# Second MoE's gate and value products by Strassen's block sums: 7 products for 8

## Chip, cores and metric

The kernel runs on one core of one Trainium2 chip. The metric is device time in microseconds (us), from launch to end; lower is better. The median of three runs stands for a kernel, and beside it there is one profiled execution, whose records are what the prediction reads.

## What is computed

Three parts follow each other: an attention with a bias made by a small network, a first mixture of experts (MoE) that takes the maximum of three products, and a second MoE that multiplies a value by a sigmoid gate.

```python
scores = scale * q @ k.T + bias           # batch 4, heads 8, sequence 576, head dim 64
x = softmax(scores) @ v                   # x: 2304 x 512
h = max(x @ w1, x @ w2, x @ w3)           # first MoE, 512 -> 768
x = h @ w_out                             # 768 -> 512
gate = 1 / (1 + exp(-(x @ w_gate)))       # second MoE, 512 -> 1536
val = x @ w_val                           # 512 -> 1536
out = (gate * val) @ w_out                # 1536 -> 512
```

The MoE weights come as 64-bit floats. The kernel decodes them to 32 bits and keeps each as two 16-bit halves, high and low.

## The kernel before

Every large product is done as three 16-bit products (high by high, high by low, low by high) that add up in one PSUM bank. The helper `mm3` (line 929, its matmuls are line 933) issues such three. The sequence of 576 tokens of a batch is worked in two halves of 288 columns, each a bank's worth.

The work is written down by a recorder (class `Recorder`): each call to an engine becomes an item with its dependences, a class of urgency (`BIAS` 0, `ATT` 1, `MOE` 2, `PREP` 3) and a cost estimate (`cost`). `emit` then sets the order on each engine by picking, among the next items of each class, the one that could start first by these estimates. Items recorded under `nc.join()` with two engines may go to either. So the order on each engine is fixed when the program is built, and an engine that comes to an item whose inputs are late waits there, with all that stands behind it.

The stages, in order of time:

- Attention, pairs of heads P = 0 to 15, four pairs per batch. `pair` loads the bias from DRAM on the SP or ACT queue (`am<-bias_d`, line 830), forms scores on TensorE, takes the maximum on VectorE (line 835) and the exponential on ScalarE (line 836). `by_pe` or `by_dma` transposes the probabilities; the DMA transposes run on the SP queue (lines 775 and 862). `value_out` makes the value product (line 878).
- First MoE, `moe1(b)`, of batch b, recorded in class MOE: it fills TensorE in the gaps of the attention of the next batch. Per batch it has 576 matmuls. Its end scales its output x and writes it as two 16-bit halves to the arena tiles `x2[b]` (lines 1008 and 1009), where all four batches stay.
- Weights of the second MoE, `split` (line 1107), after the attention has left the arena `Am`: per matrix and block of 128 columns one DMA, `decode64` (lines 543 to 545, three VectorE instructions of 512 elements), a sum of squares on ScalarE, a power-of-two scale, then the high half on ScalarE (line 1122) and the low half on VectorE (line 1123). There are 12 blocks each of gate and value weights, and 12 pieces of output weights, which need `vrel`, a scale taken from all value weights.
- Second MoE: `gate(b, m)` for 4 batches and 12 blocks m. `prod` makes the gate product and the value product, each 4 x 2 x 3 = 24 matmuls into a pair of banks. ScalarE takes the sigmoid from PSUM (line 1171), VectorE multiplies it by the value product from PSUM (line 1174), ScalarE and VectorE write the two halves (lines 1175 and 1176). `outs` makes the output product of 128 tokens, 36 matmuls of 512 columns (line 1200), put between gates by the table `between`; VectorE scales it out of PSUM (line 1205).

Of the kernel before, what the change touches and what calls it, by code (L numbers as in the profile page):

```python
# [37 lines left out]
class Mem:  # L38
# [7 lines left out]
    def region(self, ap):  # L46
# [75 lines left out]
class Recorder:  # L122
# [5 lines left out]
    DEAR = {"PE": 0.0, "DVE": 0.8, "ACT": 0.0, "POOL": 0.0, "SP": 0.0}  # L128
    NCLS = 4
# [69 lines left out]
    def cost(eng, method, out, reads, kwargs):  # L199

        n = 1
# [4 lines left out]
        if method.startswith("dma"):  # L206
# [8 lines left out]
            return (0.55 if eng == "SP" else 0.1), size / (285e3 if dram else 400e3 if size > 6e5 else 300e3) * (1.6 if parts == 64 and n > 500 else 1.0) + 0.03, 1.85  # L215
# [32 lines left out]
    def start(self, it, e):  # L248

        t = self.t_eng[e]  # L250
        for d in it.deps:
            e2, lat, own = self.ends[d]
            x = own if e2 == e == "PE" else lat
            if x > t:
                t = x
        for i in it.banks:
            for o, x in self.bank[i].items():
                if o != e and x > t:
                    t = x
# [4 lines left out]
    def choose(self, e, lists, force=False):  # L264
# [3 lines left out]
        for c in range(self.NCLS):  # L268
            ks = lists[e][c]
            seen, w = None, 0  # L270
            for it in ks:
# [7 lines left out]
                s = self.start(it, e)  # L279
# [16 lines left out]
    def emit(self):  # L296
# [15 lines left out]
        while left:  # L312
# [8 lines left out]
            calls, (busy, work, lat) = it.alts[e]  # L321
            self.t_eng[e] = s + busy
# [88 lines left out]
SIDE_CLS = ATT  # L411
PE_ALL, PE_SQ = 6, 8
# [30 lines left out]
def tile_kernel(ctx, tc, q, k, v, w1, b1, w2, mw1, mw2, mw3, mwo, gw, vw, ow, xtab, masks, out):  # L443
# [17 lines left out]
    bias_d = dram.tile([S, H, SB], F32, tag="bias_d", name="bias_d")  # L461
    PS = psum.tile([128, 4096], F32, tag="ps", name="ps")
# [29 lines left out]
    x2 = [X2[:, 2304 * b:2304 * (b + 1)].bitcast(F16).rearrange("p (e k s) -> p e k s", e=2, k=KC) for b in range(B - 1)]  # L492
# [74 lines left out]
    def up_down(src, s=None, u=None):  # L567

        g = total(src)
        e = tiny_ap().bitcast(I32)  # L570
# [44 lines left out]
    nc.sync.dma_start(wb[:, 0:1], w1.rearrange("o c -> c o").unsqueeze(0).to_broadcast([4, 32, 1]))  # L615
    nc.sync.dma_start(ytab[:, 3 * NY:], xtab[:, 3 * NY:ny])
    nc.scalar.dma_start(wb[:, 1:2], b1.rearrange("(o c z) -> o c z", o=1, z=1).to_broadcast([4, 32, 1]))
    nc.sync.dma_start(psib, xtab[:, ny + nz:ny + nz + 8 * NTAB])
    nc.sync.dma_start(msk, masks[:, 0:40])
    nc.scalar.dma_start(w2raw, w2.unsqueeze(0).to_broadcast([4, 32, H]))  # L620
# [327 lines left out]
    def moe1(b, xd, mm):  # L948
# [115 lines left out]
    common_scales()  # L1064
    mm_b = Ring([bank(6), bank(7)])
    side = first_weights((3,), Ring([X2[:, 3072 + 1536 * i:4608 + 1536 * i] for i in range(2)]), {3: X2[:, 0:3072]}, square_sum)
    for b in range(1, B):
        for P in range(PPB * b, PPB * b + PPB):
            for it in range(NIT):
# [7 lines left out]
                for _ in range(2):  # L1077
                    prep(u)
                    u += 1
                    if u >= SIDE3:  # L1080
                        next(side, None)
                if it == 1:
                    value_out(P, 0, 256, vb, pt0, True)
            value_out(P, 256, 320, vb, pt1_f if P < PE_ALL else pt1, P < PE_ALL)
            if P == PPB * b:
                with nc.at(MOE):
                    moe1(b - 1, x2[b - 1], mm_b)


    attic = Am[:, 0:3072], Am[:, 3072:7680], Am[:, 7680:13824], Am[:, 13824:19968], Am[:, 19968:22272], Am[:, 22272:23296]  # L1090
    w64_r = Ring([attic[0][:, 1024 * i:1024 * (i + 1)].bitcast(I32).rearrange("p (f t) -> p f t", t=2) for i in range(3)])
    wf_r = Ring([attic[1][:, 512 * i:512 * (i + 1)] for i in range(9)])
    GW, VW = (t.bitcast(F16).rearrange("p (e k f) -> p e k f", e=2, k=KC) for t in attic[2:4])
    x2.append(attic[4].bitcast(F16).rearrange("p (e k s) -> p e k s", e=2, k=KC))
    ob_r = Ring([attic[5][:, 512 * i:512 * (i + 1)] for i in range(2)])
    sg_r = Ring([Wm[:, S * i:S * (i + 1)] for i in range(2)])
    gT = Wm[:, 1152:14976].bitcast(F16).rearrange("p (e k s) -> p e k s", e=2, k=K2)
    OW = Wm[:, 14976:21120].bitcast(F16).rearrange("p (e k f) -> p e k f", e=2, k=K2)

    with nc.at(MOE):  # L1100
        moe1(B - 1, x2[B - 1], Ring([bank(i) for i in (0, 1, 2, 3, 5, 6, 7)]))

    scl = {nm: f32_tile([128, 2, n], nm + "_su") for nm, n in (("gw", K2), ("vw", K2), ("ow", KC))}
    vrel = f32_tile([128, K2], "vrel")
    vmn, vmx = tiny_ap(), tiny_ap()

    def split(nm, m, pieces, rel=False):

        ss = tiny_ap(len(pieces))
        fs = []  # L1110
        for i, (src, hi, lo) in enumerate(pieces):
            t, f = w64_r(), wf_r()
            nc.sync.dma_start(t.rearrange("p (k f) t -> p k f t", k=src.shape[1]), src)
            decode64(f, t)
            fv = f.rearrange("p (k f) -> p k f", k=src.shape[1])
            if rel:
                nc.vector.tensor_tensor(fv, fv, vrel[:, 4 * i:4 * i + 4].unsqueeze(2).to_broadcast([128, 4, 128]), op=ALU.mult)
            square_sum(f, ss[:, i:i + 1])
            fs.append((fv, hi, lo))
        s, _ = up_down(ss, scl[nm][:, 0, m:m + 1], scl[nm][:, 1, m:m + 1])  # L1120
        for fv, hi, lo in fs:
            nc.scalar.activation(hi, fv, AF.Copy, scale=s)
# [140 lines left out]
```

## Time and profile before

| | us |
|---|---|
| median of three runs | 1045.07 |
| lowest, highest | 1040.01, 1052.55 |
| the profiled execution | 1053.29 |
| span of its records | 1051.5 |
| TensorE busy in the span | 1014.2 |
| VectorE busy | 636.0 |
| ScalarE busy | 543.2 |
| GpSimd busy | 114.5 |

The span runs from the first to the last instruction; 1.8 us of the profiled execution lie outside it. PE is TensorE's matmuls, PEld its weight loads, DVE is VectorE, ACT ScalarE, POOL GpSimd, SP the engine that issues most DMAs. A matmul's record covers its way through the array, so matmuls overlap and 48 matmuls of 286 ns may take 6 us. L933 is line 933 of the kernel before. The changed kernel's lines lie 11 further down from line 620 to 950 or so (L830 becomes L841), and L933 becomes L944.

### The profile page before, as it was taken

Reading aid. Unit: us, or ns where it says so; the run is one execution under the profiler, and the core shown is the slowest. Engines: PE = TensorE matmul, PEld = TensorE weight load, DVE = VectorE, ACT = ScalarE, POOL = GpSimd, SP = SyncE. Lnnn points to the kernel's source line nnn. Section 1 sums busy time; section 2 is a strip of 40 time slices with the busy share of each in tenths; the row PEclk is TensorE's granted clock in tenths of the full one; section 3 lists DMA queues with packets and bytes.
Section 4 is the critical chain, followed back from the end, with each engine's and each line's share of the span. In section 5 each row is a group of like instructions: output and inputs, shape, how many; then the busy total and the mean of one; then the engine's idle time right before and its main releaser. Section 6 shows DMA issues by size and latency. Waiting matters only on the chain.

```text
span 1051.5 us, 21090 instructions
## 1 busy us (share of the span) xinstructions
PE 1014.2 (96%) x8326; PEld 687.3 (65%) x8326; DVE 636.0 (60%) x1613; ACT 543.2 (52%) x1142; POOL 114.5 (11%) x141
## 2 busy tenths in 40 slices
PE   5798998999999899999999999999999999999998
PEld 2354576665676666677778777777665666766643
DVE  5799997987888788788999929632211211221110
ACT  5899985786797777877675346422111111211100
POOL 1011132431132123121000100000000000000000
PEclk9999998999999999999999999999999999999999
DMA  7897768576999999979763401000000000000001
GB/s 197 258 306 262 258 185 187 149 190 166 206 240 171 236 223 212 224 141 237 159 190 117 158 19 61 1 1 1 11 21 21 11 11 21 1 11 11 11 21 41
DMA packets 160014, 130.02 MB, mean 124 GB/s; under 512 B 111404, under 2 KB 140332, under 8 KB 159916
## 3 DMA queue, kind: packets, MB, share of 16 engines
q1 hardware_dynamic: 157892, 121.61, 46.3%
q10 hardware_dynamic: 2024, 7.08, 2.7%
q8 instruction: 65, 1.06, 0.4%
q14 instruction: 33, 0.27, 0.1%
HBM read 89.53 MB, written 16.52 MB: 101 GB/s over the span
## 4 chain that ended last, share of the span: by engine, by line
PE 83%; DVE 8%; DMA 4%; ACT 2%; issue 1%; POOL 1%; SPq 0%; DVEq 0%; POOLq 0%; ACTq 0%
PE ps L933 48%; PE ps L1200 13%; PE ps L878 6%; PE ps L819 4%; PE ps L851 4%; PE ps L657 3%; PE ps L822 2%; DMA am<-in_k_dram 2%; DVE am L835 1%; PE ps L600 1%; PE ps L555 1%; DVE am L763 1%; DMA am<-am 1%; DMA am<-in_q_dram 1%; DMA wm<-in_xtab_dram 1%
## 5 line engine op out<-in xcount | busy, mean ns | idle before, releaser
L933 PE MATMUL ps<-wm 128*128 128x320 f16 (+2 forms) x2304 | 312.3, 288 | 0.1
L933 PEld LDWEIGHTS <-am 128*128 128x128 f16 x2304 | 225.5, 98 | 58.8
L933 PEld LDWEIGHTS <-wm 128*128 128x128 f16 x2304 | 224.7, 100 | 59.3 <-issue 6.3
L933 PE MATMUL ps<-x,am 128*128 128x288 f16 x1728 | 214.3, 286 | 0.0
L1200 PE MATMUL ps<-wm 128*128 128x512 f16 x648 | 142.0, 379 | 0.0
L836 ACT ACTIVATE am<-am,small 128x576 f32<-128x576 f32 (+1 forms) x160 | 123.2, 772 | 27.3 <-DVE small L835 23.2
L1174 DVE SCALAR_TENSOR_TENSOR wm<-ps,wm 128x576 f32<-128x576 f32 x48 | 36.4, 758 | 161.6 <-PE ps L933 160.4
L835 DVE CUSTOM_DVE_ANT_0 am<-ps,am 128x576 f32<-128x576 f32 (+1 forms) x160 | 117.8, 749 | 23.9 <-issue 11.3
L1171 ACT ACTIVATE wm<-ps,ug 128x576 f32<-128x576 f32 x48 | 35.6, 741 | 155.6 <-PE ps L933 155.4
L1200 PEld LDWEIGHTS <-wm 128*128 128x128 f16 x648 | 63.4, 98 | 74.0
L1175 ACT CAST wm<-wm 128x576 f16<-128x576 f32 x48 | 32.2, 672 | 128.7 <-DVE wm L1174 128.7
L846 POOL TENSOR_SCALAR am<-am,small 128x576 f32<-128x576 f32 (+1 forms) x60 | 60.8, 1017 | 216.6 <-DVE small L838 116.0
L878 PE MATMUL ps<-am 128*64 128x128 f32 (+4 forms) x980 | 82.1, 315 | 1.0 <-DVE wm L884 0.6
L581 ACT ACTIVATE am<-ps 128x512 f32<-128x512 f32 (+3 forms) x149 | 66.0, 466 | 24.2 <-PE ps L851 22.0
L851 PE MATMUL ps<-ident,am 128*128 128x128 f32 x450 | 71.7, 282 | 4.0 <-POOL am L846 3.1
L933 PE MATMUL ps<-am 128*128 128x288 f16 x576 | 71.2, 286 | 0.0
L1205 DVE TENSOR_TENSOR am<-ps,uo 128x512 f32<-128x512 f32 x16 | 11.1, 692 | 93.3 <-PE ps L1200 93.3
L851 PEld LDWEIGHTS ps<-ident,am 128*128 128x128 f32 x450 | 50.7, 143 | 19.5 <-POOL am L846 8.9
L819 PE MATMUL ps<-am 64*128 64x512 f16 (+1 forms) x390 | 53.6, 380 | 2.0 <-DMA am<-am 2.0
L1176 DVE TENSOR_TENSOR wm<-wm 128x576 f16<-128x576 f32 x48 | 36.4, 758 | 29.3 <-ACT wm L1175 29.3
L860 DVE SCALAR_TENSOR_TENSOR am<-am,small 128x576 f16<-128x576 f32 (+1 forms) x60 | 48.6, 832 | 7.4 <-ACT am L859 7.2
L878 PEld LDWEIGHTS ps<-am 128*64 128x64 f32 x680 | 40.3, 139 | 17.5 <-issue 3.6
(148 smaller groups left out, 1185.9 us busy)
## 6 DMA issues: line engine op xcount, KB each, us to landing
am<-bias_d SPq DMA_DIRECT2D x54, 576.0 KB, 4.6
bias_d<-am SPq DMA_DIRECT2D x36, 320.0 KB, 4.4
wm<-in_moe_w_dram SPq DMA_DIRECT2D x12, 768.0 KB, 6.1
am<-in_moe_w_gate_dram SPq DMA_DIRECT2D x12, 512.0 KB, 3.8
am<-in_moe_w_val_dram SPq DMA_DIRECT2D x12, 512.0 KB, 3.9
am<-in_moe_w_out_dram SPq DMA_DIRECT2D x12, 512.0 KB, 3.5
am<-bias_d ACTq DMA_DIRECT2D x10, 576.0 KB, 5.9
out_dram<-am SPq DMA_DIRECT2D x36, 128.0 KB, 2.3
```

The lines of the kernel that those rows point to most:

```text
L581: nc.scalar.activation(dst, src, AF.Copy, scale=scale)
L819: nc.tensor.matmul(s_main[o][:m], lhsT=q_[h, eq], rhs=k_[h, ek, 0:512], start=(i == 0), stop=(i == 2), tile_position=(64 * o, 0))
L835: nc.vector.tensor_tensor_reduce(e[:m, c], S_[o][:m], bt[:m, c], -1.0, 3.0e38, ALU.add, ALU.min, mx[:m])
L836: nc.scalar.activation(e[:m, c], e[:m, c], AF.Exp, scale=-1.0, bias=mx[:m], accum_out=l[:m, o:o + 1])
L846: nc.gpsimd.tensor_scalar(e[:m, c], e[:m, c], r[:m, o:o + 1], 1.0, op0=ALU.mult, op1=ALU.mult)
L851: nc.tensor.transpose(ps[:, t], e[:, 128 * (t0 + t):128 * (t0 + t) + 128], ident)
L860: nc.vector.scalar_tensor_tensor(ph[:m, 1, c], e[:m, c], f, ph[:m, 0, c], op0=ALU.mult, op1=ALU.subtract)
L878: nc.tensor.matmul(ps[64 * o:64 * o + 64, :N], lhsT=vv[:, o, tv], rhs=pp[:, tb], start=(i == j == 0), stop=(i == len(todo) - 1 and j == 4) ...
L933: nc.tensor.matmul(ps, lhsT=W(wp, kk), rhs=X(xp, kk), start=(first and i == 0), stop=(last and i == 2))
L1174: nc.vector.scalar_tensor_tensor(hm3(sg), pv, DOWN2, hm3(sg), op0=ALU.mult, op1=ALU.mult)
L1176: nc.vector.tensor_tensor(gT[:, 1, m, c0:c0 + S], sg, gT[:, 0, m, c0:c0 + S], op=ALU.subtract)
L1200: nc.tensor.matmul(po, lhsT=gT[:, gi, kk, 128 * ct:128 * ct + 128], rhs=OW[:, wi, kk], start=(kk == 0 and i == 0), stop=(kk == K2 - 1 and ...
```

## The change

The gate and value products now go by blocks. The weights of 256 columns (a pair i, six of them) are cut into 2 x 2 blocks of 256 x 128, the tokens of a batch into 2 x 2 blocks of 256 x 288, and the 2 x 2 block product is made from seven block products of sums and differences (Strassen's scheme in the form with 15 additions) for eight. `quad(b, i)` makes both matrices (j = 0 gate, 1 value) for a pair: 14 products of 6 matmuls, each in its own bank of a ring of six, and adds them into four 288-column results in SBUF. The sigmoid and the multiplication read these from SBUF.

- `pair_weights` makes the sums of the weights: four additions (`add2`, on VectorE or GpSimd) and high and low halves of seven blocks in place of four. `early_weights` does this for pairs 1 and 0 during the attention, from step u = 100 (pair P = 10) on, in pieces of 64 columns in `X2`; pair 1 goes to DRAM (`sw_d`) and comes back after the attention.
- `token_sums(b)` makes the seven token blocks `XC` of one batch. There is one `XC`, so it is written anew for each batch. `moe1` no longer writes halves: it stores x as 32 bits to DRAM (`x_d[b]`), and `token_sums` reads it back.
- Output products start later: the first four of batches 0 and 1 stand behind batch 1's quads. The tails of 64 tokens of two batches share one output product.
- The recorder adds 1.0 us (`LATE`) to the time at which it takes a DMA's result to be there when it picks an item, and two DMA estimates change. At the start, three small loads change queues and a ScalarE instruction without use for the result is put ahead.

```diff
-                s = self.start(it, e)
+                s = self.start(it, e, self.SPARE[e], self.LATE)
...
-    nc.sync.dma_start(wb[:, 0:1], w1.rearrange("o c -> c o").unsqueeze(0).to_broadcast([4, 32, 1]))
     nc.sync.dma_start(ytab[:, 3 * NY:], xtab[:, 3 * NY:ny])
+    nc.scalar.dma_start(wb[:, 0:1], w1.rearrange("o c -> c o").unsqueeze(0).to_broadcast([4, 32, 1]))
...
+    nc.scalar.activation(tiny_ap(), ones[:, 0:1], AF.Relu)
...
-            s, sc["ux", b] = up_down(ss)
-            for c in range(KC):
-                nc.scalar.activation(xd[:, 0, c], xf[:, c], AF.Copy, scale=s)
-                nc.vector.scalar_tensor_tensor(xd[:, 1, c], xf[:, c], s, xd[:, 0, c], op0=ALU.mult, op1=ALU.subtract)
+            sc["sx", b], sc["ux", b] = up_down(ss)
+        nc.sync.dma_start(x_d[b], xT_f[b % 2])
...
+    def add2(dst, a, b, op):
+
+        with nc.join():
+            nc.vector.tensor_tensor(dst, a, b, op=op)
+            nc.gpsimd.tensor_tensor(dst, a, b, op=op)
+
+    def halves(dst, f, s):
+
+        nc.scalar.activation(dst[0], f, AF.Copy, scale=s)
+        nc.vector.scalar_tensor_tensor(dst[1], f, s, dst[0], op0=ALU.mult, op1=ALU.subtract)
+
...
+            add2(t[:, 0], a21, a22, ALU.add)
+            add2(t[:, 1], t[:, 0], a11, ALU.subtract)
+            add2(t[:, 2], a11, a21, ALU.subtract)
+            add2(t[:, 3], a12, t[:, 1], ALU.subtract)
+            halves([W[:, 0:2, e] for e in range(2)], f[:, :, 128:256].rearrange("p (o k) f -> p o k f", o=2), s)
+            yield
+            halves([W[:, 2, e] for e in range(2)], a22, s)
+            halves([W[:, 3:7, e] for e in range(2)], t, s)
...
+                    if u >= EARLY and u % 2:
+                        next(early, None)
...
-    def gate(b, m):
-        c0 = (b % 2) * S
-        ugm = ug[:, b, m:m + 1]
-        pg = prod(GW, m, b)
...
+        for n in (1, 6, 7, 5, 2, 3, 4):
+            for j in range(2):
+                c21, c22, c11, c12 = C[j]
+                ps = part(n, j)
+                with nc.at(BIAS):
+                    if n == 1:
+                        copy_psum(c11, ps)
+                    elif n == 6:
+                        nc.vector.tensor_tensor(c12, ps, c11, op=ALU.add)
+                    elif n == 7:
+                        nc.vector.tensor_tensor(c21, ps, c12, op=ALU.add)
+                    elif n == 5:
+                        if SPLIT5:
+                            copy_psum(c22, ps)
+                            add2(c12, c22, c12, ALU.add)
+                            add2(c22, c22, c21, ALU.add)
...
+                    else:
+                        c = {2: c11, 3: c12, 4: c21}[n]
+                        nc.vector.tensor_tensor(c, ps, c, op=ALU.add)
```

VectorE's queue in the second MoE's gates and quads shows what each product leaves to it. In the kernel before, a stretch of gates some way into the second MoE (`wm<-ps,wm` is the multiplication out of PSUM, `wm<-wm` the low half):

```order
L1174 SCALAR_TENSOR_TENSOR wm<-ps,wm 128x576
L1176 TENSOR_TENSOR wm<-wm 128x576
L1170 TENSOR_SCALAR ug<-gw_su,ub 128x1
L1174 SCALAR_TENSOR_TENSOR wm<-ps,wm 128x576
L1176 TENSOR_TENSOR wm<-wm 128x576
```

In the changed kernel, part of a quad of batch 0 (`x_75` is the arena `X2`, L553 to L555 are `decode64`, L1095 is `add2`, L1196 the output weights' `vrel`):

```order
L1270 TENSOR_TENSOR x_75<-ps,x_75 128x288 x2
L1095 TENSOR_TENSOR wm<-wm 128x1024
L1272 TENSOR_TENSOR x_75<-ps,x_75 128x288 x2
L553 TENSOR_SCALAR wm<-wm 128x256 x2
L554 SCALAR_TENSOR_TENSOR wm<-wm 128x256 x2
L555 SCALAR_TENSOR_TENSOR wm<-wm 128x256
L1095 TENSOR_TENSOR x_75<-x_75 128x288
L1283 TENSOR_TENSOR x_75<-ps,x_75 128x288 x2
L555 SCALAR_TENSOR_TENSOR wm<-wm 128x256
L1283 TENSOR_TENSOR x_75<-ps,x_75 128x288
L1196 TENSOR_TENSOR wm<-wm,vrel 128x512
```

Two instructions and a small one per block have become some ten additions out of PSUM per pair, and the decoding of the output weights now stands among them.

The SP queue in the last third of the attention, before (L830 loads a bias, L862 and L775 are transposes, L714 a load of q or k):

```order
L862 DMA_TRANSPOSE am<-am 128x9x128 x2
L830 DMA am<-bias_d 128x1152
L714 DMA am<-in_q_dram 128x2x256
L716 DMA am<-in_q_dram 64x2x64
L862 DMA_TRANSPOSE am<-am 128x9x64
```

and at about the same place in the changed kernel (these are L873, L841, L725 there):

```order
L841 DMA am<-bias_d 128x1152
L1113 DMA x_75<-in_moe_w_gate_dram 128x4x128
L873 DMA_TRANSPOSE am<-am 128x9x64 x2
L725 DMA am<-in_q_dram 128x2x256
L727 DMA am<-in_q_dram 64x2x64
L786 DMA_TRANSPOSE am<-am 128x10x128
L1113 DMA x_75<-in_moe_w_gate_dram 128x4x128
```

Weight pieces of 256 KB have come in among the loads that the attention waits for; there are 16 of them, and one store of `sw_d`.

## Rows read from the trace of the kernel before

**Rows 1.** The page's 40 slices of the span: busy tenths, and granted clock in tenths.
```profile
PE   5798998999999899999999999999999999999998
DVE  5799997987888788788999929632211211221110
PEclk9999998999999999999999999999999999999999
```
**Rows 2.** Busy us by stage: PE, PEld, DVE, ACT, POOL, then PEclk, DMA share, GB/s.
```profile
325.00:350.00 25.00, 21.28 (x177) 14.22 (x176) 18.39 (x45) 15.75 (x37) 5.30 (x8) 0.93 1.03 182
...
341.00:517.00 176.00, 171.59 (x1501) 118.84 (x1501) 145.77 (x382) 132.04 (x296) 33.23 (x41) 0.99 0.98 209
...
517.00:618.00 101.00, 100.90 (x833) 80.06 (x830) 84.60 (x218) 50.76 (x110) 4.57 (x3) 1.00 0.43 135
...
670.00:1000.00 330.00, 330.00 (x2367) 231.42 (x2365) 73.97 (x120) 56.55 (x81) 0.00 (x0) 1.00 0.05 11
```
**Rows 3.** Chain that ended last, pieces in order of time: start us, us, what.
```profile
665.58 70.95 PE ps L933 x579
736.53 7.77 PE ps L1200 x36
...
1000.29 46.63 PE ps L1200 x216
```
**Rows 4.** Groups by line and form, several engines: busy us, mean ns, idle before.
```profile
L1176 DVE TENSOR_TENSOR wm<-wm 128x576 f16<-128x576 f32 x48 | 36.4, 758 | 29.3 <-ACT wm L1175 29.3
L1174 DVE SCALAR_TENSOR_TENSOR wm<-ps,wm 128x576 f32<-128x576 f32 x48 | 36.4, 758 | 161.6 <-PE ps L933 160.4 <-ACT wm L1171 0.9
...
L963 DVE SCALAR_TENSOR_TENSOR wm<-ps,small,wm 128x320 f32<-128x320 f32 x42 | 23.0, 547 | 6.2 <-PE ps L933 5.8 <-ACT am L836 0.2
...
L543 DVE TENSOR_SCALAR am<-am 128x512 int32<-128x512 int32 x36 | 14.8, 420 | 1.7 <-DMA am<-in_moe_w_out_dram 1.0 <-DMA am<-in_moe_w_val_dram 0.7
...
L1009 DVE SCALAR_TENSOR_TENSOR x<-wm,small,x 128x576 f16<-128x576 f32 x12 | 9.5, 851 | 0.0
...
L1123 DVE SCALAR_TENSOR_TENSOR am<-am,gw_su 128x512 f16<-128x512 f32 x12 | 8.9, 746 | 0.0
...
L1117 DVE TENSOR_TENSOR am<-am,vrel 128x512 f32<-128x512 f32 x12 | 8.1, 686 | 0.0
...
L1171 ACT ACTIVATE wm<-ps,ug 128x576 f32<-128x576 f32 x48 | 35.6, 741 | 155.6 <-PE ps L933 155.4
...
L555 PE MATMUL ps<-small,ones 128*128 128x1 f32 x48 | 7.7, 232 | 0.1
```
**Rows 5.** VectorE in order of time, 588 to 597 us: start us, us, what.
```profile
589.24 1.65 DVE L545 SCALAR_TENSOR_TENSOR am<-am 128x512 int32<-128x512 int32 x1
590.81 0.47 DVE L963 SCALAR_TENSOR_TENSOR wm<-ps,small,wm 128x256 f32<-128x256 f32 x1
...
594.76 0.69 DVE L544 SCALAR_TENSOR_TENSOR am<-am 128x512 int32<-128x512 int32 x1
595.37 0.54 DVE L963 SCALAR_TENSOR_TENSOR wm<-ps,small,wm 128x320 f32<-128x320 f32 x1
595.84 0.68 DVE L545 SCALAR_TENSOR_TENSOR am<-am 128x512 int32<-128x512 int32 x1
```
**Rows 6.** GpSimd in order of time, two of its six two-input additions (L974).
```profile
401.77 1.28 POOL L974 TENSOR_TENSOR wm<-wm 128x576 f16<-128x576 f32 x1 [0.31 <-ACT wm L972]
...
588.72 1.62 POOL L974 TENSOR_TENSOR wm<-wm 128x576 f16<-128x576 f32 x1 [54.95 <-ACT wm L972]
```
**Rows 7.** Start of the span in order of time, one row each of SP's queue and ScalarE.
```profile
1.54 0.67 SPq L616 DMA_DIRECT2D wm<-in_xtab_dram  x1
...
8.18 1.28 ACT L647 ACT_TABLE_LOAD   x1 [8.18 <-DMA wm<-in_xtab_dram]
```
**Rows 8.** The longest DMA pieces of the chain up to 520 us: start us, us, what.
```profile
165.96 7.17 DMA am<-in_q_dram
...
334.28 9.04 DMA am<-in_k_dram
```

More of the change, by code (lines that the diff above doesn't have):

```diff
@@ L1065, in tile_kernel, with early_weights @@
+    def early_weights():
+        raw, F, S4 = Ring(parts(X2[:, 5632:6656], [512] * 2)), Ring([X2[:, 3584:4608]]), Ring([X2[:, 4608:5632]])
+        for i in AHEAD + (0,):
+            for j in range(2):
+                yield from pair_weights(i, raw, F, S4, (j,), 64, {i: SW[0]})
+            if i:
+                nc.sync.dma_start(sw_d[i], SW_f[0])
+    early = early_weights()
     mm_b = Ring([bank(6), bank(7)])
@@ L1104, in tile_kernel @@
[L1104 to L1109, printed above, removed]
-        fs = []
[L1111 to L1117, printed above, removed]
-            square_sum(f, ss[:, i:i + 1])
[L1119 to L1122, printed above, removed]
-            nc.vector.scalar_tensor_tensor(lo, fv, s, hi, op0=ALU.mult, op1=ALU.subtract)
@@ new lines, in token_sums @@
+    def token_sums(b, lo, hi, t):
+        s = sc["sx", b]
+        for i, m in enumerate((lo, hi)):
+            nc.sync.dma_start(m, x_d[b][:, 2 * S * i:2 * S * i + 2 * S])
+        lo, hi = (m.rearrange("p (k s) -> p k s", k=2) for m in (lo, hi))
+        t = t.rearrange("p (k s) -> p k s", k=2)
+        b11, b12, b21, b22 = lo[:, :, 0:HS], lo[:, :, HS:S], hi[:, :, 0:HS], hi[:, :, HS:S]
+        put = lambda n, f: halves([XC[:, n, e] for e in range(2)], f, s)
+        put(0, b11)
+        add2(t, b22, b12, ALU.subtract)
+        add2(b12, b12, b11, ALU.subtract)
+        put(4, b12)
+        put(1, b21)
+        add2(b11, b22, b12, ALU.subtract)
+        put(5, b11)
+        put(2, b22)
+        put(6, t)
+        add2(b21, b21, b11, ALU.subtract)
+        put(3, b21)
@@ L1178, in out_rows @@
[L1178 to L1191 removed]
+            nc.vector.tensor_scalar(ugm, scl["gw"][:, 1, i:i + 1], ub[:, b:b + 1], None, op0=ALU.mult)
@@ L1193, in tile_kernel @@
+    def out_rows(pr, ct):
+        if ct == 4:
+            return [(64 * i, out[(2 * pr + i) * S + 512:(2 * pr + i + 1) * S]) for i in range(2)]
+        b, t = 2 * pr + ct // 5, ct % 5
+        r0 = b * S + t
+        return [(0, out[r0:r0 + 4 * 127 + 1:4])]
     po_r = Ring([bank(7)])
@@ L1217, in tile_kernel @@
             out_scales(b)
-        for m in range(K2):
-            gate(b, m)
-            if m in between:
-                outs(pr if b % 2 else pr - 1, between[m])
-        if b == B - 1:
-            po_r = Ring([bank(i) for i in (7, 0, 2, 5)])
-        if b % 2:
-            outs(pr, 3)
-            outs(pr, 4)
-    for ct in range(5, 9):
-        outs(1, ct)
+        for i in range(NP2):
+            quad(b, i)
+            for ct in after[b].get(i, ()):
+                outs((b if b % 2 else b - 1) // 2, ct)
@@ L1230, in tile_kernel @@
+        if b == 1:
+            po_r = Ring([bank(7), bank(4)])
+        if b < B - 1:
+            with nc.at(BIAS):
+                gx = gm_f[(1, 0, 1)[b]]
+                token_sums(b + 1, gx[:, 0:1152], gx[:, 3072:4224], gx[:, 1152:1728] if b else ob_m[:, 0:576])
+        for ct in ends[b]:
+            outs(b // 2, ct)
     with tc.manual_schedule():
```

218 lines of the change are left out of this document (148 added, 70 removed).

## The prediction

> **What bounds the kernel now.** I read the page's slices first, then the busy time by stage, the chain of waits, the groups by form, and stretches in order of time. The slices [rows 1] show TensorE full from the second slice on and VectorE at seven tenths or more until about slice 26, then at one or two. [...] The chain [rows 3] says the same: 579 matmuls of 288 columns follow without a gap in 70.95 us, so 122.5 ns each, and the 36 of an output product take 7.77 us, 216 ns each. So TensorE sets the end from 517 us on, and a matmul less there is worth its 122.5 ns, as long as the others keep up. The reader should see that this condition is the whole question: VectorE has much room after 670 us and little before.
>
> **The change part by part.** All terms are against the profiled execution: span 1051.5 us, 1053.3 with the 1.8 outside it. That execution was the slowest shown, 8.2 above the median of 1045.1; I subtract the same sum from the median.
>
> *Products.* 4 batches x 12 blocks x 48 matmuls are 2304; 4 x 6 pairs x 14 products x 6 are 2016. 288 fewer, by 122.5 ns [rows 3]: -35.3. Output products stay at 18 x 36. The column sums for scales become 13 fewer (one per chain of weights, not per block); one is two records of 0.16 us busy [rows 4], which partly overlap others: -3, between -2 and -4.
>
> *Start.* The table load of 1.28 us stood behind the wait for the first table's DMA, which was issued at 1.54 us behind another load [rows 7]. Now that DMA is first and the load is done meanwhile. The first bias activation also needs a second small table, scaled on VectorE, so I take -1, between 0 and -2.
>
> *Evictions of a quad.* TensorE needs 84 x 122.5 ns = 10.3 us for a quad. VectorE's instructions: an instruction behind another starts about 0.07 before its predecessor's recorded end (0.69 long, the next 0.61 later [rows 5]), so I take lengths less 0.07. Addition of 288 columns, half of the 0.758 of 576 [rows 4]: 0.39. Ten of them out of PSUM 3.9; two multiplications 1.4; the low half of 1024 columns about 1.2; one or two additions left to it and small ones 0.5: 7.0 us. ScalarE has four copies, two sigmoids of 0.74 [rows 4] and the high half, some 4.5. Both fit under 10.3, and a ring of six banks allows 6 x 0.735 = 4.4 us of delay. In batches 2 and 3 this costs 0.
>
> *Weights and token blocks, after the attention.* The order of the changed kernel has 684 first-MoE matmuls behind the last value product (819 before), then 984 quad matmuls without an output product between. TensorE's time: 83.8 us, then 120.5. VectorE in the first of these: eight chains of `pair_weights` (the other four are done early). A chain decodes 1024 elements, four times about 0.85 by the lengths of L543 to L545 [rows 4, 5], makes low halves of 1792 elements at 0.746 per 512 [rows 4] less the overlaps, 2.4, and about 0.85 for an addition and the scales: 6.6 each, 53 in all. The first-MoE results are 684/576 of a batch's: 24 of about 0.44 [rows 4] and half of six low halves, 15. Seven token halves at 0.74 [rows 4], 5. Together 73 of 83.8. In the second stretch I counted the queue's rows: 115 additions of 0.39 out of PSUM (45), 22 decodings of 0.85 (19), 12 multiplications by `vrel` of 0.62 [rows 4] (7), 22 of the gate (15), low halves of 1024 and other additions (17), 12 output-weight halves of 0.67 and seven token halves (13): about 118 with small ones, against 120.5. So alone VectorE would just do it.
>
> *GpSimd beside it.* The stretches also hold 26 additions of 256 and five of 576 on GpSimd, then 35 of 288, 12 of 128 and four of 576. The shortest addition of 576 there took 1.28 us [rows 6], so these are about 22 and 32 us. The trace shows what such an addition does to VectorE: one runs from 588.72 to 590.34 [rows 6], and the L545 that starts at 589.24 takes 1.65 us where its like take 0.68 [rows 5]. It ends 0.55 after the addition, as if it had begun there; the other collisions in that stage look the same. L545 has two SBUF inputs. L963, with one input in PSUM, is not seen to stretch. Two thirds of VectorE's time in the two stretches goes to instructions with two SBUF inputs or to decoding. So between none and all of GpSimd's 54 us is lost to VectorE. I take half, since an addition that comes while VectorE is out of PSUM costs nothing: 73 + 11 = 84 against 83.8, and 118 + 16 = 134 against 120.5 + 4.4 of banks. That is a wait of about 9, and I add 4, an estimate, for waits on inputs: with both engines full and the order fixed, neither catches up. **+13**, from 0 to 37 (all lost: 95 and 150, so 11 + 30 - 4). Behind a waiting VectorE stand the evictions, and TensorE waits for their banks.
>
> [...]
>
> *Early weights.* Four chains, 27 us of VectorE, 12 or so additions on GpSimd and 16 pieces of 256 KB come into the attention from P = 10 on, about 341 to 490 us. VectorE has 30 us free in 341 to 517 [rows 2], so it becomes nearly full. Where the attention gets longer, first-MoE matmuls fill TensorE: the order puts 135 more of them ahead of the last value product, 16.5 us. They are not lost, only earlier. DMA is at a share of 0.98 there [rows 2]; 4.2 MB of weights, 1.8 for `sw_d` and 1.2 for `x_d` are 7.2 MB, by 135 GB/s at 0.43 [rows 2] some 23 us of a full share. Loads the attention waits for will land later now and then. I take +5, from -4 to +23.
>
> *Change of batch.* `XC` is written anew behind the last quad's reads. From batch 0 to 1 no output product lies between, and seven halves at 0.74 share VectorE with a quad's evictions: 5.2 + 7.0 in 10.3 us. +2, from 0 to 5. The later two changes have output products of 15 us or more as cover: 0.
>
> *`LATE` and DMA estimates.* Three long DMA waits stand in the chain between 160 and 340 us, 7 to 9 us [rows 8], and with them TensorE falls to 21.3 of 25 us busy at clock 0.93 [rows 2]. Later-placed users could remove some or move them: -8 to +8, taken as 0.
>
> *Tail.* The last output products need the tails and the last quad's halves, about 6 us after its last product; their first ten of twelve blocks cover 6.5. 0.
>
> Sum: -35.3 - 3 - 1 + 13 + 5 + 2 = -19.3. Span 1032; from the median 1045.1 - 19.3, about **1026 us**.
>
> **Rivals.**
> - *TensorE stays the bound.* VectorE keeps up, the lock costs nothing, early weights are hidden: -39, about 1006, and 998 if `LATE` also removes DMA waits. For it: VectorE alone needs no more than TensorE in both stretches. Against it: [rows 5, 6].
> - *The DMA queues take it.* The early pieces find no room at a share of 0.98 [rows 2], and the 23 us fall on the attention with TensorE's queue stopped behind late loads: -19.3 - 5 + 23, about 1044, no change. For it: the three waits of 7 to 9 us [rows 8]. Against it: the weight loads are spread over some 150 us, and the first-MoE matmuls stand ready to fill.
> - *Full lock, slower.* Place: VectorE's queue from the early weights to the last output weight. If every GpSimd addition costs VectorE its whole length, the two stretches lose 37, the attention about 8 more than taken, the later quads, 7.0 + 2.8 of 10.3, some 6: -35.3 - 3 - 1 + 37 + 13 + 2 + 6 = +19, about 1064. It decides from where some five sixths of GpSimd's time is lost. Against it: a third of VectorE's time reads PSUM.
>
> **How the numbers follow.** Forecast with partial lock 0.52; TensorE as bound 0.22; DMA queues 0.15; full lock 0.11. A measurement of this kernel tells about 1%, 10 us, from no change. Faster by over 1% (below 1035): nearly all of the second, 0.9 of the forecast, a fifth of the DMA case: 0.72. Slower by over 1%: most of the full lock and a little of the DMA case: 0.10. Within 1%: 0.18. The range: 1004, where TensorE is the bound with a little from `LATE`, to 1048, the DMA case; the full lock and the best case are left out.
>
> **What would show it.** Right: 2016 matmuls of 122.5 ns in quads; gaps of TensorE in the first two batches' quads that end with VectorE, some 10 us in all, and none in batches 2 and 3; L1095, L1101 and decodings of twice their length beside GpSimd additions. The last value product near 535 us, 84 us of first-MoE matmuls behind it. Wrong: no gaps in the quads (second case), the last value product well after 550 with waits on DMAs (third), gaps throughout the quads (fourth).

## The result, and the profile after

The changed kernel takes 1053.86 us (median of 20 runs, 1048.51 to 1061.83), the kernel before 1045.27 on the same chip (20 runs, 1039.04 to 1052.99). The ratio is 1.0078, 95% interval 1.0052 to 1.0103: slower by 0.8%, which is 8.6 us, where 19.3 less were forecast. The profiled execution has a span of 1054.7 us (1056.57 with what lies around it); that of before has 1051.5. So the profiles differ by 3.2 us only: the profiled execution of before was 8 above its median, that of after 2.7.

The page of the changed kernel, the same three slices as [rows 1]:

```profile
PE   5798999988999999999999998979879999999998
DVE  6788999976878988989889878999962654855540
PEclk9999999999999999999999999999989999999999
```

In [rows 1] TensorE was at nine tenths through the second half; now it falls to seven or eight in four of slices 25 to 30, and VectorE, which ebbed away there before, stands at eight and nine up to slice 29.

The stages of after (columns as in [rows 2]; the last value product ends at 538.8, the first quad begins at 630.0, the first output product at 778.9), and three stretches of 25 us:

```profile
341.00:540.00 199.00, 194.19 (x1672) 134.78 (x1671) 175.65 (x442) 146.94 (x336) 52.14 (x57) 1.00 0.98 219
540.00:628.00 88.00, 83.60 (x676) 65.55 (x674) 75.13 (x181) 50.15 (x125) 27.34 (x26) 1.00 0.38 113
628.00:778.00 150.00, 130.97 (x1012) 100.28 (x1010) 138.60 (x296) 68.87 (x138) 46.81 (x48) 0.97 0.16 52
...
678.00:703.00 25.00, 22.21 (x179) 17.23 (x178) 24.72 (x50) 12.23 (x24) 9.66 (x8) 1.00 0.20 64
703.00:728.00 25.00, 21.58 (x172) 16.53 (x170) 24.71 (x50) 13.31 (x25) 7.93 (x8) 1.00 0.00 1
728.00:753.00 25.00, 21.28 (x170) 16.50 (x168) 24.79 (x54) 10.99 (x24) 8.68 (x8) 0.99 0.22 64
...
926.00:1012.00 86.00, 86.00 (x617) 60.28 (x617) 48.23 (x90) 24.27 (x45) 18.42 (x23) 1.00 0.04 13
```

The lost time is in the third row. Some 1012 matmuls, nearly all of them of quads, would be 124 us at the 122.5 ns of [rows 3] and take 150. VectorE is busy 138.6 of them, and between 678 and 753 it has 0.2 to 0.3 us free in each 25: it is the engine that ends last there. From 926 on TensorE is full again.

The chain that ended last, from the first outputs on (start us, us, what):

```profile
780.52 10.67 PE ps L1313 x35
...
792.66 7.77 PE ps L1313 x36
...
851.04 20.58 PE ps L1258 x168
...
1011.99 38.86 PE ps L1313 x180
```

168 matmuls in 20.58 us are 122.5 ns each and an output product is 7.77 us: the pace of [rows 3], so quads cost nothing beyond their matmuls in batches 2 and 3. The first row is 35 output matmuls in 10.67 us instead of 7.6: right behind the stretch in which it waited, TensorE ran slower (mean granted clock 0.83 from 778 to 803).

What TensorE waited for between 625 and 800 us (us in total, times, longest):

```profile
PE ps L565 <- ACT junk L598: 9.5, 4, 3.8
PE ps L1258 <- DVE x L1283: 3.0, 4, 1.3
PE ps L1258 <- DVE wm L1283: 2.1, 3, 1.2
PE ps L1258 <- DVE am L1101: 1.9, 2, 1.5
```

Nearly half is not at a bank of a quad but at the column sums of the output weights (L565): four matmuls that need ScalarE's squares, these need VectorE's decoding, and while TensorE stands at one, the quads behind it in its queue stand too. By group, over the whole span (busy us, mean ns, idle before):

```profile
L1258 PE MATMUL ps<-am 128*128 128x288 f16 x1680 | 213.4, 289 | 4.8 <-DVE wm L1283 2.1 <-DVE x L1283 0.8 <-DVE x L1272 0.7
L1313 PE MATMUL ps<-wm 128*128 128x512 f16 x648 | 145.0, 385 | 3.3 <-ACT wm L1100 1.4 <-DVE wm L1101 1.0 <-DVE wm L1095 1.0
L1258 PE MATMUL ps<-am,x 128*128 128x288 f16 x336 | 42.8, 286 | 4.3 <-DVE x L1283 2.2 <-DVE am L1101 1.9
L565 PE MATMUL ps<-small,ones 128*128 128x4 f32 (+2 forms) x86 | 15.4, 250 | 15.1 <-ACT junk L598 10.1 <-ACT junk L1115 4.7 <-DVE small L1120 0.2
```

TensorE in all is busy 987.7 us (1014.2 before) and idle 67.0 of the span (37.3 before): 26.5 us of work gone, 29.7 of waiting come, which makes the 3.2. VectorE has gone from 636.0 to 802.9 us, GpSimd from 114.5 to 259.0.

### The profile page after: what moved, and what is told of

The parts are those of the page before. It is cut to its first block, busy times and chain, and to the rows that moved or that the text cites. A ratio compares the mean times of both kernels' runs of the same rounds, so it can differ in the third digit from the quotient of the medians.

```text
span 1054.7 us, 21403 instructions
## 1 busy us (share of the span) xinstructions
PE 987.7 (94%) x8012; PEld 657.6 (62%) x8012; DVE 802.9 (76%) x1934; ACT 602.0 (57%) x1303; POOL 259.0 (25%) x288
## 4 chain that ended last, share of the span: by engine, by line
PE 35%; DVE 18%; issue 4%; ACT 2%; DMA 1%; POOL 0%; DVEq 0%; POOLq 0%; ACTq 0%; SPq 0%
PE ps L1313 13%; PE ps L1258 13%; PE ps L944 6%; DVE am L1101 2%; DVE x L1283 1%; PE ps L889 1%; DVE wm L554 1%; DVE wm L974 1%; DVE wm L555 1%; DVE wm L1095 1%; DVE wm L553 1%; DVE x L1095 1%; DVE am L846 1%; PE ps L830 1%; DVE wm L1101 1%
## 5 line engine op out<-in xcount | busy, mean ns | idle before, releaser
L944 PE MATMUL ps<-wm 128*128 128x320 f16 (+2 forms) x2304 | 307.2, 286 | 1.3 <-ACT wm L591 0.9
L1258 PE MATMUL ps<-am 128*128 128x288 f16 x1680 | 213.4, 289 | 4.8 <-DVE wm L1283 2.1
L1258 PEld LDWEIGHTS <-am 128*128 128x128 f16 x1680 | 165.9, 99 | 51.4 <-issue 7.0
L846 DVE CUSTOM_DVE_ANT_0 am<-ps,am 128x576 f32<-128x576 f32 (+1 forms) x160 | 117.3, 748 | 23.2 <-issue 13.0
L857 POOL TENSOR_SCALAR am<-am,small 128x576 f32<-128x576 f32 (+1 forms) x64 | 64.9, 1019 | 191.2 <-DVE small L849 116.3
L1096 POOL TENSOR_TENSOR x<-x 128x288 f32<-128x288 f32 (+2 forms) x80 | 75.5, 950 | 132.9 <-ACT x L591 57.3
L1096 POOL TENSOR_TENSOR wm<-wm 128x288 f32<-128x288 f32 (+3 forms) x40 | 40.4, 1011 | 169.9 <-ACT wm L591 61.7
L862 PE MATMUL ps<-ident,am 128*128 128x128 f32 x450 | 72.8, 282 | 8.5 <-POOL am L857 6.3
L862 PEld LDWEIGHTS ps<-ident,am 128*128 128x128 f32 x450 | 51.1, 143 | 28.4 <-POOL am L857 10.7
L830 PE MATMUL ps<-am 64*128 64x512 f16 (+1 forms) x390 | 56.8, 384 | 7.0 <-DMA am<-am 5.5
L591 ACT ACTIVATE wm<-ps 128x288 f32<-128x288 f32 x56 | 22.5, 402 | 69.2 <-PE ps L1258 59.9
L591 ACT ACTIVATE x<-ps 128x288 f32<-128x288 f32 x72 | 28.4, 404 | 50.6 <-PE ps L1258 48.2
L974 DVE SCALAR_TENSOR_TENSOR wm<-ps,small,wm 128x256 f32<-128x256 f32 (+1 forms) x84 | 43.0, 512 | 12.7 <-PE ps L944 11.1
L1283 DVE TENSOR_TENSOR x<-ps,x 128x288 f32<-128x288 f32 x108 | 46.4, 447 | 5.2 <-PE ps L1258 4.9
```

The source lines that it names most:

```text
L591: nc.scalar.activation(dst, src, AF.Copy, scale=scale)
L830: nc.tensor.matmul(s_main[o][:m], lhsT=q_[h, eq], rhs=k_[h, ek, 0:512], start=(i == 0), stop=(i == 2), tile_position=(64 * o, 0))
L846: nc.vector.tensor_tensor_reduce(e[:m, c], S_[o][:m], bt[:m, c], -1.0, 3.0e38, ALU.add, ALU.min, mx[:m])
L857: nc.gpsimd.tensor_scalar(e[:m, c], e[:m, c], r[:m, o:o + 1], 1.0, op0=ALU.mult, op1=ALU.mult)
L862: nc.tensor.transpose(ps[:, t], e[:, 128 * (t0 + t):128 * (t0 + t) + 128], ident)
L944: nc.tensor.matmul(ps, lhsT=W(wp, kk), rhs=X(xp, kk), start=(first and i == 0), stop=(last and i == 2))
```

## The experiments

Two theories. **V**: the gain was there and was spent on VectorE; between the attention and the first outputs its work takes longer than TensorE's, and TensorE waits at its results. **L**: VectorE's own work would fit, and what costs the time is GpSimd's additions, which hold VectorE up. This holding up, seen at the L545 of [rows 5, 6], is what the prediction and the expectations call the lock. Others are named where they are tested. Each run stands beside runs of the kernel before on the same chip (1043.9 to 1044.7).

**e1: less decoding of output weights.** In `out_weights`:

```
-                decode64(f[...], t)
+                nc.vector.tensor_scalar(f[...].bitcast(I32), t[..., 1], 3, 0x3FFFFFFF, ...)
```

> The changed kernel, with two of the three decoding instructions left out for the output weights (48 VectorE instructions of 256 elements, 26 us of recorded length in the profile of the changed kernel); the output weights lose their signs and three low bits. Theory V (VectorE's work between the last value product and the last output weight sets the time there): about 1054 - 20 to 26, so 1028 to 1034, and the stretch of 984 quad matmuls falls from 150 to about 127 us. Rival A (the loss lies in the attention, through the early weights): 1050 to 1056. Rival P (the planner's edits lost it): 1050 to 1056.

Measured 1042.5 (10 runs), ratio 0.9987 (0.9953 to 1.0021): 11 us less than the changed kernel, half of what was expected. VectorE's busy time fell by 18.7 us (802.9 to 784.2). The order of TensorE's queue changed with it: the first output product came after 840 quad matmuls, where the changed kernel has all 984 in front, so the expected 127 us of that stretch can't be compared.

**e2: no weights made in the attention.** `EARLY = 100` becomes `EARLY = 1000`.

> The changed kernel with no weights decoded during the attention: all six pairs come after it. Theory V: four chains, 27 us of VectorE, move into the stretch where VectorE is the bound, and the attention gets up to 12 us back: 1062 to 1076. Rival A: the attention gets back what it lost and little is lost behind it: 1038 to 1046. Rival P: 1050 to 1060.

1068.1 (4 runs), ratio 1.0244 (1.0190 to 1.0299). The early weights were worth 14 us. Between first quad and first output VectorE is now busy 153.7 of 162 us, 15 more in a stretch that is 12 longer. The attention is not what loses the time.

**e3: the planner's numbers undone.** `LATE = 0.0` and the old DMA costs (three numbers) in the changed kernel.

> The changed kernel with the recorder's edits undone (LATE 0, the old DMA estimates); the start stays changed. Rival P: 1038 to 1046. Theory V and rival A: 1050 to 1058, no different from the changed kernel by more than 4 us.

1057.3 (4 runs), ratio 1.0130 (1.0073 to 1.0186). These numbers are not the cause.

**e4: no GpSimd in the second MoE.** In `add2`:

```
-            nc.gpsimd.tensor_tensor(dst, a, b, op=op)
```

> The changed kernel with every addition of add2 on VectorE, none on GpSimd. VectorE gets about 30 us of additions of its own between the last value product and the end of batch 1's quads, and loses the waits beside GpSimd there (some 24 us of stretched instructions in the changed kernel's profile). Theory V with the lock: the two nearly cancel, 1052 to 1064. If GpSimd's additions cost VectorE nothing: 1075 to 1085. If they cost it their whole length (54 us): 1028 to 1036.

1056.0 (10 runs), ratio 1.0099 (1.0062 to 1.0135): no gain. The shape of the loss changed, though. The stages (columns as above):

```profile
628.00:778.00 150.00, 126.05 (x1011) 99.45 (x1008) 139.88 (x342) 71.11 (x138) 0.00 (x0) 0.93 0.16 52
...
725.00:750.00 25.00, 25.00 (x207) 19.99 (x205) 23.81 (x62) 12.47 (x25) 0.00 (x0) 1.00 0.13 43
750.00:775.00 25.00, 6.28 (x49) 4.81 (x46) 21.43 (x59) 7.50 (x18) 0.00 (x0) 0.69 0.30 95
775.00:800.00 25.00, 19.73 (x83) 9.04 (x84) 11.01 (x30) 4.57 (x9) 0.00 (x0) 0.77 0.03 11
```

Without GpSimd TensorE runs its quads nearly in full until 755 and then stands twice at a column sum of the output weights, 13.3 us the second time:

```profile
PE ps L565 <- ACT junk L598: 21.6, 2, 13.3
```

The stretch is 150 us long again and VectorE is busy 139.9 of it, against 138.6. The mean granted clock fell to 0.69 and 0.77 around these waits.

The rows of the two kernels show why both come to the same. In the stretch from 628 to 778, after:

```profile
L554 DVE SCALAR_TENSOR_TENSOR wm<-wm 128x256 int32<-128x256 int32 x24 | 14.3, 602 | 0.2
L553 DVE TENSOR_SCALAR wm<-wm 128x256 int32<-128x256 int32 x24 | 10.7, 462 | 0.0
L1095 DVE TENSOR_TENSOR x<-x 128x288 f32<-128x288 f32 x8 | 7.0, 870 | 0.7 <-POOL x L1096 0.7
L1101 DVE SCALAR_TENSOR_TENSOR am<-wm,small,am 128x576 f16<-128x576 f32 x6 | 6.5, 1103 | 0.0
L1096 POOL TENSOR_TENSOR x<-x 128x288 f32<-128x288 f32 x26 | 24.4, 946 | 22.4 <-ACT x L591 14.9 <-DVE wm L554 3.5 <-DVE ug L1251 2.0
```

and in e4 (its L1100 is L1101 there):

```profile
L1095 DVE TENSOR_TENSOR x<-x 128x288 f32<-128x288 f32 x34 | 14.6, 450 | 0.1
L554 DVE SCALAR_TENSOR_TENSOR wm<-wm 128x256 int32<-128x256 int32 x24 | 10.0, 420 | 0.3
L553 DVE TENSOR_SCALAR wm<-wm 128x256 int32<-128x256 int32 x24 | 6.8, 286 | 0.8 <-DMA wm<-in_moe_w_out_dram 0.7
L1100 DVE SCALAR_TENSOR_TENSOR am<-wm,small,am 128x576 f16<-128x576 f32 x6 | 4.8, 808 | 0.0
```

The same instruction takes 602 ns on average in the kernel with GpSimd's additions and 420 in the one without, 462 and 286, 870 and 450, 1103 and 808. With the smaller groups of the stretch this is 18.2 us lost by VectorE, 39% of GpSimd's 46.8. What GpSimd took over would have cost VectorE 33 additions of 0.45, 11 of 0.28 and 4 of 0.75: 21.0 us. It gives 21 and takes 18.

**e5: e4 and e1 together.**

> [...] Theory V (VectorE's own work is too much for the stretch behind the attention, and the loss to GpSimd roughly equals what GpSimd takes over): against the run with the decoding alone left out (1042.5) it gains little or nothing, 1036 to 1046. Rival L (the lock alone is what is lost, and moving additions failed only because the decoding then came too late): 1022 to 1032, with TensorE without a gap from the first quad to the end.

1038.77 (10 runs), ratio 0.9962 (0.9932 to 0.9992): within V's range and not in L's. It is 3.7 below e1, with intervals that overlap.

**e6: less decoding in the attention.** The edit of e1, for the chains of `early_weights`.

> Two of the three decoding instructions of the two weight chains that are made during the attention are left out (32 instructions of 64 x 4 columns, some 15 us of VectorE; their values are then wrong). If those chains hold up the attention through VectorE, the last value product comes 8 to 12 us earlier than in the changed kernel (553) and the run ends 6 to 12 us earlier (1042 to 1048). If TensorE is what bounds the attention (97% busy between 341 and 553), it moves by under 3 us and the run is at 1050 to 1056.

1059.7 (4 runs), ratio 1.0155 (1.0098 to 1.0212). Not faster, which is the second case's direction, but slower than either case said, 5.8 above the changed kernel where under 3 was expected. The 553 of the expectation was misread: the last value product ends at 538.8 in the changed kernel, and before 542 here, while VectorE did 12.0 us less between 341 and 540 (163.65 for 175.65).

**e7: the ratios folded into the scale.** In `out_weights`:

```
-            nc.vector.tensor_tensor(f..., f..., vrel[:, 2 * i:2 * i + 2]..., op=ALU.mult)
...
-            halves([... 4 * i:4 * i + 4 ...], f, scl_o[:, 0, c:c + 1])
+        nc.vector.tensor_scalar(sv, vrel, scl_o[:, 0, c:c + 1], None, op0=ALU.mult)
+            for a in range(2):
+                halves([... k:k + 2 ...], f[:, 256 * a:256 * a + 256], sv[:, 2 * i + a:2 * i + a + 1])
```

> The 12 multiplications of the output weights by the ratios between value weights' scales are taken off VectorE, the ratio is put into the scale of the splitting instead (24 halves of 256 columns where 12 of 512 were); the output is the same. About 6 us of VectorE leave the stretch behind the attention, and the square sums wait for nothing but the decoding. Theory V: 1044 to 1051. If TensorE's waits come from the order of its queue and not from VectorE's amount of work: 1051 to 1056.

1047.83 (10 runs), ratio 1.0020 (0.9986 to 1.0054): 6 us less than the changed kernel for 5.4 us less on VectorE (797.5), as V expected, and level with the kernel before.

**e8: a third pair made early.** `AHEAD = (1, 2)`, `EARLY = 70`.

> Three pairs of gate and value weights instead of two are made during the attention (the third kept in DRAM like the second), from a little earlier on. Theory V with room on VectorE in the attention: some 12 us of VectorE leave the stretch behind it and the run ends 6 to 12 us earlier, 1042 to 1048. If the attention has no room left on VectorE (88% busy in its second half), the last value product comes 6 to 12 us later and the run stays at 1050 to 1062.

1064.62 (4 runs), ratio 1.0202 (1.0150 to 1.0254): above both ranges, on the side of the second case. Between 340 and 564 TensorE waits 7.5 us for first-MoE results that VectorE has late (three waits, the longest 6.3), the last value product comes 24 us later and the first quad at 643. Neither fewer (e2) nor more (e8) early weights do better than the changed kernel's two pairs.

**e9: as little on VectorE as the program allows.** e5 and e7, and the edit of e1 in `pair_weights` behind the attention.

> VectorE's work between the first part and the outputs is cut as far as the program's shape allows: two of the three decoding instructions of all gate, value and output weights that are made after the attention are left out (their values are then wrong), the multiplications by the ratios are folded away, and GpSimd adds nothing. Theory V: TensorE is without a gap behind the first quad, its work there is 391 us (24 quads and 18 outputs at full clock), and the run ends 22 to 30 us before the changed kernel, 1024 to 1032, which is what the 288 products less are worth. If waits remain that are not VectorE's amount (column sums in TensorE's order, clock), it stays at 1036 to 1044.

1028.05 (4 runs), ratio 0.9853 (0.9798 to 0.9908), as V expected. The same stretch, from just before its first quad (621.9) to its first output (748.6; columns of the stages), and below it its quads (columns of the groups):

```profile
620.00:748.00 128.00, 123.69 (x1011) 98.53 (x1010) 117.28 (x307) 68.41 (x141) 0.00 (x0) 1.00 0.18 60
```

```profile
L1262 PE MATMUL ps<-am 128*128 128x288 f16 x1680 | 208.0, 286 | 0.0
...
L1262 PE MATMUL ps<-am,x 128*128 128x288 f16 x336 | 42.3, 286 | 2.7 <-ACT am L1099 1.6 <-DVE am L1100 1.0
```

128 us for 150, TensorE full but for 4.3, and quads of 250.3 us instead of 256.2. The products of the kernel before, by group:

```profile
L933 PE MATMUL ps<-x,am 128*128 128x288 f16 x1728 | 214.3, 286 | 0.0
...
L933 PE MATMUL ps<-am 128*128 128x288 f16 x576 | 71.2, 286 | 0.0
```

These are 285.5 us, so the 288 matmuls less are worth 35.2 in e9.

**e10: e7 without GpSimd.**

> The fold of e7 and no GpSimd additions in the second MoE; the output is the same. Theory V (the loss to GpSimd equals what it takes over): 1043 to 1051, as e7. Rival L (the lock is a loss of its own): 1036 to 1043.

1049.87 (10 runs), ratio 1.0062 (1.0025 to 1.0099): as V expected, not better than e7.

**e11: column sums later in TensorE's order.** e7 with `SPARE = {"PE": 1.5, ...}`.

> The fold of e7, and the planner takes results of other engines 1.5 us later for TensorE than it did, so that column sums stand later in TensorE's queue. If the order of that queue (waits at column sums while quads behind them could run) is what the stretch loses, TensorE's waits at column sums fall from 8 to under 3 us and the run ends at 1039 to 1044; under theory V the waits only move to other instructions, 1045 to 1051.

1073.11 (4 runs), ratio 1.0266 (1.0215 to 1.0318): a miss of both expectations. The number moved every instruction of the planner's order; the first quad came at 650 instead of 630. In the stretch the waits at L598's squares were 7.2 us, against 8.1, so they did not go. How much the fixed order alone costs stays open.

**e12: two decoding instructions for three.** e7, and in both weight functions `decode64` without its last instruction, the one that puts in `lo >> 29`.

> The fold of e7, and the second MoE's weights are decoded by two instructions instead of three: the lowest three of 23 bits of each weight are left out (a relative error of up to 2^-20 in a weight). Some 25 us of VectorE less than e7, 17 of them before the last output weight. Theory V: 1031 to 1039, faster than the kernel before by about 1%. If VectorE's amount is not the bound any more once the fold is made: 1043 to 1048.

1037.91 (10 runs), ratio 0.9945 (0.9916 to 0.9973), in V's range. VectorE: 770.3 us. As in e1, the order changed: the first output product came after 882 quad matmuls.

**e13: the same shorter decoding in the kernel before.**

> The kernel before, with the second MoE's weights decoded by two instructions (the lowest three bits left out), as in e12: 36 instructions of some 0.7 us less on VectorE, about 25 us, all between 517 and 736 us. Theory V says that VectorE is the bound of the changed kernel alone: here TensorE is full in that stretch, so nothing changes, 1040 to 1047, ratio 0.996 to 1.002. If the shorter decoding is worth 8 us or more by itself, 1032 to 1038, and e12's gain says nothing on the block sums.

1043.76 (10 runs), ratio 0.9983 (0.9949 to 1.0017). Its VectorE has 21.2 us less to do (614.8), most of them here:

```profile
518.00:736.00 218.00, 217.49 (x1766) 171.70 (x1765) 124.26 (x320) 95.38 (x189) 4.00 (x2) 1.00 0.20 64
```

and in the kernel before:

```profile
518.00:736.00 218.00, 217.38 (x1779) 172.77 (x1777) 146.45 (x362) 99.74 (x196) 4.57 (x3) 1.00 0.22 69
```

22 us of VectorE gone from this stretch and TensorE as full as it was. The same cut that gives the changed kernel 6 to 10 us over e7 (the medians of e15 and e12) gives the kernel before 0.9 us of its median. The interval of e13 would still allow 5; that TensorE is as full as it was is the firmer sign.

**e14: e12 without GpSimd.**

> e12 without GpSimd's additions in the second MoE. Theory V with half of GpSimd's time lost on VectorE: 1035 to 1042, as e12. If the lock is a loss of its own, once VectorE has a little room: 1027 to 1033.

1034.89 (10 runs), ratio 0.9915 (0.9882 to 0.9949): a hair below V's range and 2 above that of the lock, the fastest kernel here that leaves out no part of the work but those three bits. Its stretch (columns of the stages):

```profile
622.00:760.00 138.00, 124.55 (x1010) 98.65 (x1008) 125.65 (x328) 69.27 (x144) 0.00 (x0) 0.97 0.17 56
```

138 us. TensorE stands once, 9.5 us at the last column sum of the output weights, as in e4 but shorter.

**e15: e12 again.**

> e12 once more, beside e13 and e14 on one chip, for a narrower interval: 1035 to 1041, ratio 0.991 to 0.997.

1041.33 (12 runs), ratio 0.9983 (0.9953 to 1.0012): outside what was expected, 3.4 us above e12 of the same kernel. Over both, 22 runs, the median is 1039.8. So differences of 3 to 4 us between single kernels of this list should not be leaned on; e14 beats e15 by 6.4 beside it, and e5 is 3.7 under e1, while leaving GpSimd out gained nothing in e4 and e10. So where VectorE has less to do, leaving GpSimd out may be worth some 3 to 6 us: theory L is refuted at the size expected of it in e5 and e10, not down to nothing.

## Why the prediction was wrong

Its mechanism was in it, sized too small. By the profiles the forecast was a span of 1032 and the measured one is 1054.7. The 22.7 us lie in two places: the first quad at 630.0 instead of 618.8 (535 + 83.8), and the stretch from there to the first output, 149.0 us instead of 135.5 (120.5 + 13 + 2); behind it some 2 came back. Some 5 more in the medians come from subtracting the sum from the median, while the profile it was made against was 8 above the median.

- **Products, -35.3.** Right where TensorE is kept fed: 35.2 in e9. In the changed kernel it is 29.3, 256.2 for 285.5. The term was priced at full pace in a stretch where TensorE, by the sum's next term, was to wait; the 1012 matmuls there (some column sums among them) had 129.4 ns of busy time each, not 122.5. The row behind the stretch, 10.67 us for 35 output matmuls, is of the same kind.
- **Column sums, -3.** 15.4 us for 18.5: right in busy time. What was missed is that the remaining ones stand in TensorE's queue in front of quads and wait there for VectorE, 9.5 us.
- **Weights and token blocks, +13. This is the step that failed.** From first quad to first output it took 149.0 us, 28.5 over TensorE's 120.5, where 13 and the 2 of the batch change were said. VectorE's work was counted well, 134 with half of the lock; 138.6 were measured. What it lost to GpSimd's additions was too: I took half of their time, an estimate from the stretched L545 of [rows 5, 6], and against e4 it is 39%, of a longer time (46.8 us, not 32; part of that is GpSimd's own wait for VectorE, see the last section). But the sum then let VectorE's 134 us end 9 us behind TensorE's 125 and added 4 "since neither catches up". VectorE, with as much work as the stretch is long, did not run without gaps: it was idle 11.4 of the 150 us, and in the same stretch 8.3 of 162 in e2, 10.1 of 150 in e4, 10.3 of 132 in e5, 6.7 of 140 in e7, 12.5 of 148 in e10, 5.4 of 142 in e11, 12.4 of 138 in e14. The stretch is VectorE's work and 5 to 13 us more. Of the 11.4, VectorE waited 4.9 for quad products, 1.5 for a column sum, 1.6 for ScalarE and 1.9 for GpSimd, and the rest went in short gaps: it waits for TensorE while TensorE waits for it. In e9, with 117.3 us of VectorE's work, TensorE is idle 4.3 of the 128 and VectorE 10.7, so there TensorE is the longer one.
- **Early weights, +5, and the stage behind the attention.** The last value product ended at 538.8, 4 later than the 535 said. Behind it TensorE was to be full and was 83.6 of 88 us busy, 4.4 lost, about 3 of them at column sums of pair weights; e9 has no such loss (81.6 of 82 between 538 and 620). Some 4 more are idle time before 340 us, 32.0 for 27.7. The waits that grew there are at GpSimd's results (5.0 for 2.5 us) and at a DMA (5.5 for 2.0). Why is open: among the other kernels with the changed program this idle time lies between 27.6 and 34 without a pattern, and at 44.0 in e11.
- **Start, -1.** The table load now ends at 3.8 us and the first bias activation begins at 8.07, where the load ended at 9.46 before [rows 7]. TensorE has 254 matmuls in the first 40 us, 231 before, in less busy time (23.65 for 24.95, at a granted clock of 1.00 for 0.96). By 340 us the lead is gone, 2971 matmuls for 2991.
- **Evictions of a quad, batch change, `LATE`.** Evictions are as said: 20.58 us for two quads in batches 2 and 3. Waits at the token blocks of the next batch (L1101 in the waits) are 1.9 for the +2. The change to batch 3, taken as 0, cost 1.0 (TensorE busy 27.04 of 28 us from 898 to 926). Without `LATE` e3 is 3.4 slower, which its interval does not tell from the 0 said.

Of the rivals, TensorE as the bound did not come. e9, which comes near it, is at 1028, not 1006: in its profile (1022.8, 5 under its median) TensorE still ends 395 us after its first quad (621.9 to 1017.0), where 387 would be matmuls at full pace, and 5 of the 8 are its waits. The DMA queues did not take it: no wait on a DMA is among TensorE's waits behind 340 us, though three weight loads of 2.7, 3.1 and 3.5 us stand in the chain between 539 and 618. The full lock at 1064 had the right sign, but its size is refuted by e4.

The rows of e4 and of the changed kernel show which instructions GpSimd's additions stretched: L554, with two SBUF inputs, from 420 to 602 ns, and L553, with one, from 286 to 462. L1283, which reads PSUM, takes 447 ns in the changed kernel and 450 in e4. What makes the two engines wait for each other no run here shows. A VectorE instruction caught in the act (start us, us, what):

```profile
734.47 2.38 POOL L1096 TENSOR_TENSOR x<-x 128x288 f32<-128x288 f32 x2
734.72 0.88 DVE L553 TENSOR_SCALAR wm<-wm 128x256 int32<-128x256 int32 x1
...
736.12 1.01 DVE L554 SCALAR_TENSOR_TENSOR wm<-wm 128x256 int32<-128x256 int32 x1
...
738.86 0.28 DVE L553 TENSOR_SCALAR wm<-wm 128x256 int32<-128x256 int32 x1
```

0.88 beside GpSimd, 0.28 four us later alone. So the additions given to GpSimd were nearly worthless in the changed kernel, and leaving them out nearly free.

What is shown: taking VectorE's work away behind the attention gives time back in the changed kernel (e1, e5, e7, e9, e12), though not inside the attention (e6), and none that can be told from nothing in the kernel before (e13); moving it from GpSimd to VectorE (e4, e10), out of the attention (e2) or further into it (e8) does not. What stays open is how VectorE's gaps divide between the planner's fixed order and real dependences, for each of these edits also changes that order and the one run on it, e11, missed; and the 4 us in the first part.

A version that beats both is e14, 0.85% (0.51 to 1.18%) under the kernel before, at the price of three bits of each weight. With the output unchanged, e7 is level with the kernel before and no better.

## What to carry to other kernels

Matmuls saved by block sums are paid in additions on the engine that drains PSUM, so read that engine's free time in the very stretch where the sums are made, not over the span: here, in the kernel before, VectorE had 256 us free from 670 to 1000 and 16 in the 101 behind the attention [rows 2]. Where two engines come out about level in a sum, forecast the longer one plus its own gaps (5 to 13 us in 130 to 160 here), and price the other engine's work at its pace after waits (129.4 ns for a matmul of 122.5 here). Work given to a helper that holds the first engine up counts only by what it takes over less what it holds up (21.0 and 18.2 us here), and both can be read by leaving the helper out once.

## What the runs showed of the hardware

VectorE and GpSimd hold each other up here, and in the two pairs below the one that began first goes through. In the changed kernel (start us, us, what):

```profile
720.35 0.43 POOL L1096 TENSOR_TENSOR wm<-wm 128x128 f16<-128x128 f32 x1 [5.43 <-ACT wm L1294]
720.46 1.40 DVE L1095 TENSOR_TENSOR wm<-wm 128x1024 f16<-128x1024 f32 x1
...
731.62 1.22 DVE L1095 TENSOR_TENSOR wm<-x,wm 128x1024 f16<-128x1024 f32 x1
731.69 1.44 POOL L1096 TENSOR_TENSOR wm<-x,wm 128x128 f16<-128x128 f32 x1 [5.50 <-ACT wm L1294]
```

GpSimd's 128 columns take 0.43 us where it began first and 1.44 where VectorE did; VectorE's 1024 columns take 1.40 and 1.22, and 1.22 on average in e4, without GpSimd. So the mean of 0.92 to 0.94 us for 128 columns in the stretch, as long as for 288 (0.80 to 0.95, where VectorE alone needs 0.45), is not GpSimd's own pace: it holds waits for VectorE.

And a wait of TensorE cost more than its length: in e4 the granted clock was 0.69 and 0.77 on average in the two stretches of 25 us around waits of 8.3 and 13.3 us, while the stretch before them had 1.00, and in the changed kernel the first 35 output matmuls behind its waits took 10.67 us instead of 7.6, at 0.83 from 778 to 803.
